# Weighting q before its transposes for the first four token tiles, and pairing the feed-forward units of both token halves

## The chip, the core and the metric

The kernel runs on one core of a Trainium2 chip. Its engines are TensorE (PE in the profile, with its weight loads as PEld), VectorE (DVE), ScalarE (ACT), GpSimd (POOL) and SyncE (SP); each works through its own instructions in order. Data comes from and goes to device memory by DMA, issued from the queues of SP, POOL and, once, ACT. The metric is device time of one execution in microseconds.

## The reference

Attention with a cosine weighting and no softmax, and behind it a gated feed-forward layer:

```python
theta = pi / 2 * arange(S) / S                       # S = 576
phi(x) = concat([relu(x) * cos(theta), relu(x) * sin(theta)], axis=-1)
kv  = einsum('bhsf,bhsd->bhfd', phi(k), v)           # B = 8, H = 8, D = 64
z   = sum over s of phi(k)
x   = einsum('bhsf,bhfd->bhsd', phi(q), kv) / (einsum('bhsf,bhf->bhs', phi(q), z) + 1e-6)
x   = x with the heads side by side: 4608 tokens x 512
out = (silu(x @ w_gate) * (x @ w_val)) @ w_out       # 512 -> 1536 -> 512
```

Inputs and output are float32. The kernel computes in bf16 with float32 sums.

## The kernel before

**Tokens.** A batch's 576 positions are held as 64 partitions times 9 *slots* (position = 9 p + c for partition p and slot c). Two heads, e = 0 and 1, share the 128 partitions; the four head pairs are g = 0 to 3, taken two at a time as j = 0, 1 with i = g mod 2. A *token tile* t is two neighbouring slots of all eight heads, 128 tokens; tile 4 takes the last slot of batch 0 and the first of batch 1. Four tiles make a token group of 512, `tg`, of which there are nine.

**Attention.** `relu_k` makes relu(k), `vmul` multiplies v by cos and sin and appends the weights themselves, so that `kv_mm` gives kv and z in one product; `kv_out` copies it from PSUM into `kvd`, a matrix in which the blocks for other heads are zero. The weights of q are applied late: `qturn_pe` transposes q's slots on PE and the relu that copies them out of PSUM gives `qt`; `a_half(t, j)` multiplies `qt` by `kvd` into 2 x 260 columns, ACT scales the cosine half into `tmp` (L278), and DVE scales the sine half and adds it, giving `num` (L279). `x_norm` divides by the denominator: `den` (L287), `rec` (L289) and `x` in two halves (L293). `x_turn` transposes x on PE (L309), and ACT copies it into `xT` (L310), or, later in the kernel, it does so by DMA.

**Feed-forward.** `ffn_fc(tg, fc, lo, hi)` is a *unit*: for one of 12 column blocks fc, the products with w_gate and w_val (L329) over slots lo to hi of a token group, silu on ACT (`sg`, L337), the product on DVE (`ht`, L339). `ffn_out` multiplies `ht` by w_out (L355) and copies the sum as `ob` (L362), on ACT for even tiles and on DVE for odd ones, for SP to write out.

**PSUM.** All eight banks are one tile; `take(n)` hands them out round robin, n at a time and aligned, skipping those that are held. The kv product is held until `kv_free`, an output sum until its last piece is issued. A bank that is handed out again is written once its earlier readers are through.

**Order.** It is written out by hand. q and v of batch 0 come by SP in float32 (`first_q`, the first `CUT[0]` = 4 slots, and `first_v`), the rest by POOL with a cast to bf16, in the order of the calls: w0, ..., w5 are pairs of column blocks of w_gate and w_val (`load_w`), wo0 to wo2 thirds of w_out (`load_wo`). `idle_products(n)` issues n products of zeros, used by nothing. For token group 0 the units are split into halves: a0 to a11 are the units of tiles 0 and 1, b0 to b11 those of tiles 2 and 3. `order` lists them and `at(slot, ...)` hangs other work behind one; a slot (piece, t) stands behind a third of output tile t. In `order` before, a0 to a5 come first, and then the b units with the rest of a between them; a0 and a1 are themselves split into a quarter for tile 0 and one for tile 1. From token group 1 on, units take 512 tokens. PE takes up everything in this order.

Of the kernel before, what the change touches and what calls it, by code (L numbers as in the profile page):

```python
# [17 lines left out]
def kernel(  # L18
# [10 lines left out]
    nc = tc.nc  # L29
    B, H, S, D = q.shape  # L30
    P = 128
    G = H // 2
    J = G // 2
# [50 lines left out]
    def raw_of(b, nm):  # L84
        if (b, nm) not in raws:
            raws[b, nm] = raw.tile([P, G, NC, D], BF16, name=f"raw_{nm}")
        return raws[b, nm]

    def load(b, nm, parts=1):
        t, sv, n = raw_of(b, nm), source(b, nm), G // parts  # L90
        for i in range(parts):
            sl = slice(i * n, (i + 1) * n)
            nc.gpsimd.dma_start(out=t[:, sl].rearrange("p g c d -> p g (c d)"), in_=sv[:, sl])  # L93

    def load_slots(b, nm, lo, hi):
        nc.gpsimd.dma_start(out=raw_of(b, nm)[:, :, lo:hi].rearrange("p g c d -> p g (c d)"),
                            in_=source(b, nm)[:, :, lo * D:hi * D])
# [4 lines left out]

    def load_first(nm, gs, cs=slice(0, NC)):
        if nm not in first:
            first[nm] = consts.tile([P, G, NC, D], FP32, name=f"first_{nm}")
        nc.sync.dma_start(out=first[nm][:, gs, cs].rearrange("p g c d -> p g (c d)"),  # L106
                          in_=source(0, nm)[:, gs, cs.start * D:cs.stop * D])

# [20 lines left out]
    def idle_products(n):  # L129
        ps = take(1)  # L130
        for _ in range(n):
            nc.tensor.matmul(out=ps, lhsT=zeros, rhs=zeros.unsqueeze(1).to_broadcast([P, 4, P]), start=True, stop=True)  # L132

    idle_products(24)


    rad = math.pi / 2.0 / S
# [48 lines left out]
    def relu_op(eng, out, in_):  # L186
        if eng == "act":
            nc.scalar.activation(out=out, in_=in_, func=AF.Relu)  # L188
        else:
            nc.vector.tensor_single_scalar(out=out, in_=in_, scalar=0.0, op=ALU.max)  # L190

    def relu_k(b, lo, hi, eng):
        o = raw_of(b, "k")[:, lo:hi]
        relu_op(eng, o, o)
# [6 lines left out]
    def vmul(b, g):  # L201
        nc.vector.tensor_tensor(  # L202
            out=v2s[b % 2][:, g, :, :, 0:D],
            in0=(first if b == 0 and g < 2 else {"v": raw_of(b, "v")})["v"][:, g].unsqueeze(2).to_broadcast([P, NC, 2, D]),
            in1=tab, op=ALU.mult,
        )
# [37 lines left out]
    def kv_out(b, engs=("act", "dve"), js=slice(0, J)):  # L244
        ps = st[b, "kvps"]
        for e, eng in enumerate(engs):
            for i in range(2):
                hs = slice(i * D, (i + 1) * D)
                (nc.scalar.copy if eng == "act" else nc.vector.tensor_copy)(  # L249
                    out=kvd[b % 2][hs, e, js, :, i].rearrange("p j w x -> p (j w) x"),  # L250
                    in_=ps[hs, e, js.start * 2 * D1:js.stop * 2 * D1].rearrange("p (y x) -> p y x", x=D1))

    def kv_free(b):
        held.pop(("kv", b))

    xT = {}

# [83 lines left out]
    def ffn_fc(*a):  # L341
        ffn_mm(*a)
        ffn_act(*a)
# [36 lines left out]
                                                        in_=ob[e * SH:(e + 1) * SH, 0:hi - lo])  # L380


    for i in range(5):
        load_w(i)
    load(1, "k")
    load(1, "v", 2)
    load_w(5)
    load_slots(1, "q", 0, CUT[1])
    for i in range(3):
        load_wo(i)  # L390
    load_slots(1, "q", CUT[1], NC)
    for nm in ("k", "v", "q"):
        load(2, nm)

# [4 lines left out]
    def at(s, *fns):  # L399
        plan.setdefault(s, []).extend(fns)  # L400
# [5 lines left out]
    def a_(t, j):  # L406
        return lambda: (a_half(t, j), x_norm(t) if j else None)

    def turn(t, fast=False):
        return lambda: x_turn(t, fast)  # L410

    def q_(b, j, part, eng="act"):
        lo, hi = ((0, CUT[b]), (CUT[b], NC))[part]
        return lambda: qturn_pe(b, j, lo, hi, eng)


    def relu_first_q(j, cs, eng):
        sl = slice(2 * j, 2 * j + 2)
        relu_op(eng, raw_of(0, "q")[:, sl, cs], first["q"][:, sl, cs])

    def relu_first_q(j, eng):
        sl = (slice(None), slice(2 * j, 2 * j + 2), slice(0, CUT[0]))
        relu_op(eng, raw_of(0, "q")[sl], first["q"][sl])

    vmul(0, 0)
    vmul(0, 1)
    for g in (2, 3):
        nc.scalar.copy(out=raw_of(0, "v")[:, g], in_=first["v"][:, g])
        vmul(0, g)
    for j in range(J):  # L430
        relu_first_q(j, "act")
    for j in range(J):
        q_(0, j, 0)()
    relu_k(0, 0, 2, "dve")
    idle_products(2)
    kv_mm(0, 0)
    idle_products(2)
    kv_out(0, js=slice(0, 1))
    relu_k(0, 2, 4, "dve")
    for t in range(2):  # L440
        a_(t, 0)()
    kv_mm(0, 1)
    idle_products(3)
    kv_out(0, js=slice(1, 2))
    kv_free(0)
    for t in range(2):
        a_(t, 1)()
    q_(0, 0, 1)()
    idle_products(6)
    x_turn(0, fast=True)  # L450
    q_(0, 1, 1)()
    idle_products(2)
    for f in range(2):
        ffn_fc(0, f, 0, 2)
    a_(2, 0)()
    x_turn(1, fast=True)
    a_(2, 1)()


    order = [("a", f) for f in range(6)]  # L460
    for f in range(FC):
        order.append(("b", f))
        if f in (0, 1, 3, 4, 7, 8):
            order.append(("a", {0: 6, 1: 7, 3: 8, 4: 9, 7: 10, 8: 11}[f]))
    at("a0", a_(3, 0))
    at("a1", a_(3, 1))
    at("a3", turn(2, True))
    at("a5", turn(3, True))
    at("b2", lambda: relu_k(1, 0, 2, "dve"))
    at("a9", lambda: relu_k(1, 2, 4, "dve"))  # L470
    for g in range(G):
        at(f"b{4 + g}", lambda g=g: vmul(1, g))
    at("a10", lambda: kv_mm(1, 0))
    at("a11", lambda: kv_mm(1, 1), lambda: kv_out(1))
    at("b10", lambda: kv_free(1))
    at("b9", q_(1, 0, 0))
    at("b10", q_(1, 1, 0), a_(4, 0))
    at("b11", a_(4, 1))
    at((0, 0), a_(5, 0), q_(1, 0, 1))
    at((0, 1), a_(5, 1), q_(1, 1, 1))  # L480
    at((0, 2), turn(4, True))
    at((0, 3), a_(6, 0))
    at((1, 0), turn(5, True), a_(6, 1))
    at((1, 2), a_(7, 0), turn(6, True))
    at((1, 3), a_(7, 1))
    at((2, 1), turn(7, True))
    HALF = GH // 2
    for nm, f in order:
        ffn_fc(0, f, *((HALF, GH) if nm == "b" else (0, HALF) if f > 1 else (2, HALF)))
        slot(f"{nm}{f}")  # L490
    for piece in range(3):
        for t in range(OUT):
# [76 lines left out]
```

## Time and profile before

| | us |
|---|---|
| median of 6 runs | 339.83 |
| lowest and highest run | 338.48 and 341.64 |
| the profiled execution, device time | 340.66 |
| its span, first to last instruction | 338.8 |
| PE busy in the span | 328.9 |
| DVE, ACT, POOL busy | 189.3, 158.1, 32.3 |
| first unit of token group 0 starts | 20.00 |
| unit b0 starts | 29.54 |
| token group 1 starts | 63.32 |

The profile counts time from the first instruction. The span is shorter than the device time, which takes in what lies before and after it. Busy time of PE overstates its work, since a matmul's end is modelled and overlaps the next one; what PE truly spends is seen from the starts of successive matmuls.

### The profile page before, as it was taken

Reading aid. Unit: us, or ns where it says so; the run is one execution under the profiler, and the core shown is the slowest. Engines: PE = TensorE matmul, PEld = TensorE weight load, DVE = VectorE, ACT = ScalarE, POOL = GpSimd, SP = SyncE. Lnnn points to the kernel's source line nnn. Section 1 sums busy time; section 2 is a strip of 40 time slices with the busy share of each in tenths; the row PEclk is TensorE's granted clock in tenths of the full one; section 3 lists DMA queues with packets and bytes.
Section 4 is the critical chain, followed back from the end, with each engine's and each line's share of the span. In section 5 each row is a group of like instructions: output and inputs, shape, how many; then the busy total and the mean of one; then the engine's idle time right before and its main releaser. Section 6 shows DMA issues by size and latency. Waiting matters only on the chain.

```text
span 338.8 us, 5965 instructions
## 1 busy us (share of the span) xinstructions
PE 328.9 (97%) x2299; PEld 165.7 (49%) x2299; DVE 189.3 (56%) x426; ACT 158.1 (47%) x309; POOL 32.3 (10%) x50
## 2 busy tenths in 40 slices
PE   8789999999999999999999999999999999999995
PEld 3358865454445444444444444544444445444443
DVE  6385855589725962596259714981478147714320
ACT  6564464678425741584157514851354135413321
POOL 9454320002002000200000000000000000000000
PEclk9999999999999999999999999999999999999999
DMA  8999999998985928492810172017301410141013
GB/s 237 196 197 203 206 206 207 234 220 137 157 157 88 167 38 172 67 183 48 155 41 16 34 149 62 15 31 135 75 18 31 98 44 15 32 110 31 0 33 93
DMA packets 57085, 36.76 MB, mean 109 GB/s; under 512 B 31329, under 2 KB 52065, under 8 KB 57057
## 3 DMA queue, kind: packets, MB, share of 16 engines
q0 software_dynamic: 20624, 18.03, 33.5%
q1 hardware_dynamic: 36272, 18.23, 25.8%
q8 instruction: 18, 0.29, 0.4%
q10 hardware_dynamic: 160, 0.13, 0.1%
q14 instruction: 11, 0.08, 0.1%
HBM read 37.75 MB, written 9.44 MB: 139 GB/s over the span
## 4 chain that ended last, share of the span: by engine, by line
PE 91%; DMA 3%; DVE 2%; ACT 2%; issue 1%; SPq 0%; ACTq 0%
PE banks L329 56%; PE banks L355 26%; PE banks L268 5%; PE banks L237 3%; DMA first_q<-in_q_dram 3%; DVE x L293 1%; DVE num L279 1%; ACT tmp L278 1%; PE banks L223 1%; PE banks L373 0%; PE banks L309 0%; ACT raw_q L188 0%; ACT xT L310 0%; PE banks L132 0%; SPq L106 0%
## 5 line engine op out<-in xcount | busy, mean ns | idle before, releaser
L329 PE MATMUL banks<-xT,wg_sb 128*128 128x512 bf16 (+2 forms) x488 | 113.5, 355 | 2.2 <-DVE ht L339 0.8
L329 PE MATMUL banks<-xT,wv_sb 128*128 128x512 bf16 (+2 forms) x488 | 113.3, 355 | 0.0
L339 DVE TENSOR_TENSOR ht<-sg,banks 128x512 bf16<-128x512 bf16 (+2 forms) x122 | 76.1, 624 | 66.0 <-PE banks L329 50.8
L337 ACT ACTIVATE sg<-banks 128x512 bf16<-128x512 f32 (+2 forms) x122 | 66.9, 548 | 89.9 <-PE banks L329 87.5
L355 PE MATMUL banks<-wo_sb,ht 128*128 128x512 bf16 x420 | 93.6, 379 | 0.0
L329 PEld LDWEIGHTS <-wv_sb 128*128 128x128 bf16 x488 | 47.2, 98 | 46.3
L329 PEld LDWEIGHTS <-wg_sb 128*128 128x128 bf16 x488 | 45.7, 98 | 39.1 <-issue 3.6
L355 PEld LDWEIGHTS <-ht 128*128 128x128 bf16 x420 | 40.7, 98 | 46.4 <-issue 0.4
L362 DVE COPY ob<-banks 128x512 f32<-128x512 f32 x17 | 11.8, 691 | 55.2 <-PE banks L355 55.1
L278 ACT ACTIVATE tmp<-banks,cst 128x260 f32<-128x260 f32 x72 | 34.1, 476 | 15.5 <-PE banks L268 15.4
L279 DVE SCALAR_TENSOR_TENSOR num<-banks,cst,tmp 128x260 f32<-128x260 f32 x72 | 34.8, 484 | 9.2 <-ACT tmp L278 8.9
L362 ACT COPY ob<-banks 128x512 f32<-128x512 f32 x18 | 10.6, 586 | 55.0 <-PE banks L355 55.0
L268 PE MATMUL banks<-kvd,qt 128*128 128x260 bf16 (+1 forms) x160 | 27.8, 276 | 0.4 <-DVE kvd L249 0.2
L293 DVE TENSOR_TENSOR x<-num,rec 128x256 bf16<-128x256 f32 x72 | 27.4, 421 | 1.2
L202 DVE TENSOR_TENSOR v<-raw_v,tab 128x1152 bf16<-128x1152 bf16 x30 | 22.3, 752 | 0.0
L268 PEld LDWEIGHTS <-qt 128*128 128x128 bf16 (+1 forms) x160 | 13.3, 100 | 17.0 <-issue 3.3
L188 ACT ACTIVATE raw_k<-raw_k 128x576 bf16<-128x576 bf16 x24 | 16.0, 675 | 0.0
L188 ACT ACTIVATE r_q<-raw_q 128x576 bf16<-128x576 bf16 x24 | 16.0, 675 | 0.0
L93 POOL DMA_DIRECT2D raw_k<-in_k_dram x9 | 7.0, 780 | 87.1 <-issue 82.7
L132 PE MATMUL banks<-zeros 128*128 128x512 bf16 x39 | 12.3, 469 | 1.0 <-DVE zeros L127 1.0
L237 PEld LDWEIGHTS <-raw_k 64*64 64x64 bf16 x576 | 8.8, 106 | 6.2 <-issue 5.3
L237 PE MATMUL banks<-v,raw_k 64*64 64x130 bf16 x576 | 11.5, 220 | 0.0
(45 smaller groups left out, 98.0 us busy)
## 6 DMA issues: line engine op xcount, KB each, us to landing
out_dram<-ob SPq DMA_DIRECT2D x70, 128.0 KB, 2.4
raw_k<-in_k_dram POOLq DMA_DIRECT2D x7, 576.0 KB, 12.0
raw_v<-in_v_dram POOLq DMA_DIRECT2D x6, 576.0 KB, 13.4
raw_q<-in_q_dram POOLq DMA_DIRECT2D x6, 576.0 KB, 15.5
wg_sb<-in_moe_w_gate_dram POOLq DMA_DIRECT2D x6, 256.0 KB, 10.6
wv_sb<-in_moe_w_val_dram POOLq DMA_DIRECT2D x6, 256.0 KB, 10.8
wo_sb<-in_moe_w_out_dram POOLq DMA_DIRECT2D x3, 512.0 KB, 14.9
first_v<-in_v_dram SPq DMA_DIRECT2D x2, 576.0 KB, 4.1
```

Source lines behind the costliest of these rows:

```text
L188: nc.scalar.activation(out=out, in_=in_, func=AF.Relu)
L202: nc.vector.tensor_tensor(out=v2s[b % 2][:, g, :, :, 0:D], in0=(first if b == 0 and g < 2 else {"v": raw_of(b, "v")})["v"][:, g].unsqueeze ...
L237: nc.tensor.matmul(out=ps[i * D:(i + 1) * D, e, j * 2 * D1:(j + 1) * 2 * D1], lhsT=raws[b, "k"][es, g, c], rhs=v2s[b % 2][es, g, c, :, 0:D ...
L268: nc.tensor.matmul(out=ps[ms, e, 0:4 * D1], lhsT=st[b, "qt"][:, e, j, c:c + n].rearrange("p c s -> p (c s)"), rhs=kvd[b % 2][:, e, j].rear ...
L278: nc.scalar.activation(out=tmp, in_=av[:, :, 0], func=AF.Copy, scale=cst[:, c0, 0:1])
L279: nc.vector.scalar_tensor_tensor(out=st["num", t][:, j], in0=av[:, :, 1], scalar=cst[:, c0, 1:2], in1=tmp, op0=ALU.mult, op1=ALU.add,)
L293: nc.vector.tensor_tensor(out=x[:, 4 * j * D:(4 * j + 4) * D].rearrange("p (i e d) -> p e i d", i=2, e=2), in0=num[:, hs, 0:D].rearrange(" ...
L329: nc.tensor.matmul(out=o, lhsT=w[:, kc, fs], rhs=xT[tg][:, kc, ts], start=(kc == 0), stop=(kc == KC - 1))
L337: nc.scalar.activation(out=sg[:, 0:n], in_=ps[0], func=AF.Silu)
L339: nc.vector.tensor_tensor(out=ht[:, fc, r:r + n], in0=sg[:, 0:n], in1=ps[1], op=ALU.mult)
L355: nc.tensor.matmul(out=o_ps[t], lhsT=ht[:, fc, r:r + P], rhs=wo_sb[:, fc], start=(fc == 0), stop=(fc == FC - 1))
L362: (nc.scalar.copy if t % 2 == 0 else nc.vector.tensor_copy)(out=ob, in_=ps)
```

## The change

For tiles 0 to 3 q is weighted first: `weight_q(c, w, eng)` makes relu(q) times the cosine (w = 0) or sine (w = 1) of one slot in one instruction, on ACT or DVE, into `qw`. `turn_qw(t)` transposes both, and ACT and DVE copy one each into `qwT`. `a_tile(t)` multiplies both by their parts of `kvd` and adds them in PSUM, and DVE divides straight from PSUM with one `den`, one `rec` and one `x` for the tile. The ninth slot of batch 0 still goes through `qturn_pe`, now behind b1. The order becomes pairs, two a units and two b units in turn; all of column blocks 0 and 1 for tiles 0 and 1 comes before it. Loads, v products, kv products and the tiles 4 to 7 hang at other slots, and the numbers of products of zeros differ (24, 2, 2, 3, 6 and 2 before; 28, 2, 4 and 3 after).

```diff
-            first[nm] = consts.tile([P, G, NC, D], FP32, name=f"first_{nm}")
+            first[nm] = consts.tile([P, G, cs.stop, D], FP32, name=f"first_{nm}")
...
-    idle_products(24)
+    idle_products(28)
...
+    NW = 8
+    qw = consts.tile([P, 2, J, NW, 2, D], BF16)
+    qwT = {}
+
+    def weight_q(c, w, eng):
+        o, sc = qw[:, w, :, c], csk[:, c, w:w + 1]
+        i = (first["q"] if c < CUT[0] else raw_of(0, "q"))[:, :, c].rearrange("p (j i) d -> p j i d", i=2)
+        if eng == "act":
+            nc.scalar.activation(out=o, in_=i, func=AF.Relu, scale=sc)
+        else:
+            nc.vector.tensor_scalar(out=o, in0=i, scalar1=sc, scalar2=0.0, op0=ALU.mult, op1=ALU.max)
+
+    def turn_qw(t):
+        qwT[t] = consts.tile([P, 2, 2, J, 2, SH], BF16, name=f"qwT_{t % 2}")
+        for w, eng in enumerate(("act", "dve")):
+            ps = take(1).bitcast(BF16).rearrange("p (y e s) -> p y e s", e=2, s=SH)
+            for j in range(J):
+                for c in range(2):
+                    nc.tensor.transpose(out=ps[:, 2 * j + c].rearrange("p e s -> p (e s)"),
+                                        in_=qw[:, w, j, 2 * t + c].rearrange("p i d -> p (i d)"), identity=ident)
+            (nc.scalar.copy if eng == "act" else nc.vector.tensor_copy)(
+                out=qwT[t][:, w].rearrange("p e j c s -> p (j c) e s"), in_=ps[:, 0:2 * J])
+
+    def a_tile(t):
+        ps = take(2)
+        for e in range(2):
+            for j in range(J):
+                for w in range(2):
+                    nc.tensor.matmul(
+                        out=ps[:, e, 2 * j * D1:2 * (j + 1) * D1],
+                        lhsT=qwT[t][:, w, e, j].rearrange("p c s -> p (c s)"),
+                        rhs=kvd[0][:, e, j, w].rearrange("p i x -> p (i x)"),
+                        start=(w == 0), stop=(w == 1),
+                    )
...
+        nc.vector.tensor_single_scalar(out=dv, in_=num[:, :, :, D:D1], scalar=1e-6, op=ALU.add)
...
+        nc.vector.reciprocal(out=rec, in_=den)
...
+        nc.vector.tensor_tensor(
+            out=x.rearrange("p (y e d) -> p e y d", e=2, d=D), in0=num[:, :, :, 0:D],
...
-    for i in range(5):
+    for i in range(4):
         load_w(i)
     load(1, "k")
+    load_w(4)
+    load_w(5)
     load(1, "v", 2)
-    load_w(5)
     load_slots(1, "q", 0, CUT[1])
-    for i in range(3):
-        load_wo(i)
+    load_wo(0)
+    load_wo(1)
     load_slots(1, "q", CUT[1], NC)
+    load_wo(2)
...
-    for j in range(J):
-        relu_first_q(j, "act")
-    for j in range(J):
-        q_(0, j, 0)()
+    for c in range(CUT[0]):
+        weight_q(c, 0, "act")
+        weight_q(c, 1, "dve")
     relu_k(0, 0, 2, "dve")
-    idle_products(2)
+    turn_qw(0)
     kv_mm(0, 0)
     idle_products(2)
+    relu_k(0, 2, 4, "dve")
+    turn_qw(1)
     kv_out(0, js=slice(0, 1))
-    relu_k(0, 2, 4, "dve")
-    for t in range(2):
-        a_(t, 0)()
     kv_mm(0, 1)
-    idle_products(3)
+    idle_products(4)
     kv_out(0, js=slice(1, 2))
     kv_free(0)
-    for t in range(2):
-        a_(t, 1)()
-    q_(0, 0, 1)()
-    idle_products(6)
+    a_tile(0)
+    a_tile(1)
+    idle_products(3)
+    for c in (4, 5):
+        weight_q(c, 0, "act")
+        weight_q(c, 1, "act")
     x_turn(0, fast=True)
-    q_(0, 1, 1)()
-    idle_products(2)
+    turn_qw(2)
+    for c in (6, 7):
+        weight_q(c, 0, "act")
+        weight_q(c, 1, "dve")
+    a_tile(2)
     for f in range(2):
         ffn_fc(0, f, 0, 2)
-    a_(2, 0)()
     x_turn(1, fast=True)
-    a_(2, 1)()
+    turn_qw(3)
+    for f in range(2):
+        ffn_fc(0, f, 2, 4)
+    x_turn(2, fast=True)
+    a_tile(3)
...
-    order = [("a", f) for f in range(6)]
-    for f in range(FC):
-        order.append(("b", f))
-        if f in (0, 1, 3, 4, 7, 8):
-            order.append(("a", {0: 6, 1: 7, 3: 8, 4: 9, 7: 10, 8: 11}[f]))
-    at("a0", a_(3, 0))
-    at("a1", a_(3, 1))
-    at("a3", turn(2, True))
-    at("a5", turn(3, True))
-    at("b2", lambda: relu_k(1, 0, 2, "dve"))
+    order = []
+    for f in range(0, FC, 2):
+        order += [("a", g) for g in (f + 2, f + 3) if g < FC]
+        order += [("b", g) for g in (f, f + 1)]
+    at("a3", turn(3, True))
+    for j in range(J):
+        at("b1", lambda j=j: qturn_pe(0, j, NC - 1, NC, "act"))
+    at("a8", lambda: relu_k(1, 0, 2, "dve"))
     at("a9", lambda: relu_k(1, 2, 4, "dve"))
-    for g in range(G):
-        at(f"b{4 + g}", lambda g=g: vmul(1, g))
-    at("a10", lambda: kv_mm(1, 0))
-    at("a11", lambda: kv_mm(1, 1), lambda: kv_out(1))
-    at("b10", lambda: kv_free(1))
-    at("b9", q_(1, 0, 0))
-    at("b10", q_(1, 1, 0), a_(4, 0))
-    at("b11", a_(4, 1))
-    at((0, 0), a_(5, 0), q_(1, 0, 1))
-    at((0, 1), a_(5, 1), q_(1, 1, 1))
-    at((0, 2), turn(4, True))
-    at((0, 3), a_(6, 0))
-    at((1, 0), turn(5, True), a_(6, 1))
-    at((1, 2), a_(7, 0), turn(6, True))
+    for g, s in enumerate(("a10", "a11", "b8", "b9")):
+        at(s, lambda g=g: vmul(1, g))
+    at("b9", lambda: kv_mm(1, 0))
+    at("b10", lambda: kv_mm(1, 1), lambda: kv_out(1))
+    at("b11", q_(1, 0, 0), q_(1, 1, 0))
+    at((0, 0), lambda: kv_free(1), a_(4, 0))
+    at((0, 1), a_(4, 1))
+    at((0, 2), a_(5, 0))
+    at((0, 3), a_(5, 1))
+    at((1, 0), turn(4, True), q_(1, 0, 1), a_(6, 0))
+    at((1, 1), a_(6, 1), q_(1, 1, 1))
+    at((1, 2), turn(5, True), a_(7, 0))
     at((1, 3), a_(7, 1))
-    at((2, 1), turn(7, True))
+    at((2, 0), turn(6, True))
+    at((2, 2), turn(7, True))
     HALF = GH // 2
     for nm, f in order:
-        ffn_fc(0, f, *((HALF, GH) if nm == "b" else (0, HALF) if f > 1 else (2, HALF)))
+        ffn_fc(0, f, *((HALF, GH) if nm == "b" else (0, HALF)))
         slot(f"{nm}{f}")
```

More of the change, by code (lines that the diff above doesn't have):

```diff
@@ L254, in kv_free @@
         held.pop(("kv", b))
+    NW = 8
[29 more added lines that the diff above has]
+                    )
+        num = ps[:, :, 0:2 * J * D1].rearrange("p e (y x) -> p e y x", x=D1)
+        den = smp.tile([P, H, 1], FP32, name="den")
+        dv = den.rearrange("p (e y) o -> p e y o", e=2)
+        nc.vector.tensor_single_scalar(out=dv, in_=num[:, :, :, D:D1], scalar=1e-6, op=ALU.add)
+        rec = smp.tile([P, H, 1], FP32, name="rec")
+        nc.vector.reciprocal(out=rec, in_=den)
+        x = xp.tile([P, d_model], BF16, name="x")
+        nc.vector.tensor_tensor(
+            out=x.rearrange("p (y e d) -> p e y d", e=2, d=D), in0=num[:, :, :, 0:D],
+            in1=rec.rearrange("p (e y) o -> p e y o", e=2).to_broadcast([P, 2, 2 * J, D]), op=ALU.mult,
+        )
+        st["x", t] = x
     xT = {}
@@ L414, in q_ @@
         return lambda: qturn_pe(b, j, lo, hi, eng)
[L417 to L423, printed above, removed]
     vmul(0, 0)
```

## The prediction

> **What bounds the kernel now.** Three views, in this order: the busy table and slices, the chain that ended last, and TensorE's timeline around the stages that the diff edits.
>
> ```profile
> PE 328.9 (97%) x2299; PEld 165.7 (49%) x2299; DVE 189.3 (56%) x426; ACT 158.1 (47%) x309; POOL 32.3 (10%) x50
> PE 91%; DMA 3%; DVE 2%; ACT 2%; issue 1%; SPq 0%; ACTq 0%
> ```
>
> TensorE (PE) is the bound: the chain is 91% PE. After 63.32 us no row shows PE waiting, so what the edited part saves comes off the end in full, and only the first 63 us matter. There the chain runs:
>
> ```profile
> 1.75 8.51 DMA first_q<-in_q_dram
> ...
> 18.12 0.77 DVE x L293 x2
> 18.89 0.04 issue
> 18.94 0.29 PE banks L309 x2
> ...
> 28.91 0.59 ACT xT L310
> 29.50 0.04 issue
> 29.54 11.51 PE banks L329 x104
> ```
>
> Nothing starts before q lands at 10.26; the first x is ready at 18.89; PE is dense from 29.54, where unit b0 begins. The stretches from there:
>
> ```profile
> 29.54:47.12 17.58, 17.58 (x232) 14.78 (x232) 10.63 (x25) 8.10 (x21) 7.23 (x10) 1.00 1.29 204
> 47.12:63.32 16.20, 15.67 (x107) 7.84 (x105) 9.81 (x27) 9.02 (x18) 0.74 (x1) 1.00 1.21 208
> ```
>
> (Columns: stretch, length, busy PE, weight loads, DVE, ACT, POOL, clock, DMA share, GB/s.) The first is full. The second, one unit and the twelve output pieces, has holes that busy time partly hides, because a matmul's modelled end overlaps the next:
>
> ```profile
> 56.89 0.39 PE L268 MATMUL banks<-kvd,qt 128*128 128x260 bf16 x2
> 57.43 0.62 PE L309 MATMUL banks<-ident,x 128*128 128x128 bf16 x4
> ...
> 58.97 1.89 PE L355 MATMUL banks<-wo_sb,ht 128*128 128x512 bf16 x8
> 61.13 0.62 PE L309 MATMUL banks<-ident,x 128*128 128x128 bf16 x4 [0.27 <-DVE x L293]
> ```
>
> Two matmuls of 260 columns stream in 0.22, so PE stood 0.32 before 57.43; eight of 512 stream in 1.73, so 0.43 before 61.13. With 0.24 inside each of these turns and 0.17 before 54.95, about 1.4 us are stalls.
>
> **What the Trainium skill says.** "ScalarE: Activation LUTs", What ACT_TABLE_LOAD costs: each per-partition pointer operand adds about 93 ns. The trace agrees: tmp, 128x260 with a pointer scale, 478 ns; sg, 128x256, 384. "VectorE: DVE Perf Modes", the perf-mode tier table: one-source fp32 SBUF operations can run at 2x, those from PSUM at most 2x, tensor_tensor from PSUM at 1x. Agreement: the tab cast, 1152 fp32, took 0.76 (0.16 + 1152 x 0.52 ns); x, 256 from fp32, 421 ns (0.155 + 267). No row shows a bf16 PSUM copy on DVE. "TensorE: Matmul & The Clock Gate", Part 1: the array runs at half clock until some 3.4 us of activity, and again after an idle window of that length. The trace shows the start of it: products of zeros 0.43 apart until 6.9, then 0.22.
>
> **The change, part by part.** *Early stage.* The two relu of q (0.62 each), 32 of 36 q transposes, the four qt relu, eight tmp (0.478) and eight num (0.485) of tiles 0 to 3 go. Added: 16 weightings, 32 transposes of 128 columns (four take 0.22), eight qwT copies, and per tile one den (0.21) and rec (0.20) and one x of 512 instead of two of 256. The matmuls stream the same 16 x 260 columns. Prices: ACT weighting as tmp, 0.48, 0.39 apart; DVE weighting 0.16 + 256 x 0.52 = 0.29, 0.21 apart (1x: 0.42 and 0.34); qwT on ACT as the 128x512 xT copy, 0.58; on DVE between 0.42 (2x) and 0.69 (the fp32 ob copy); x of 512, 0.155 + 533 = 0.69. At the low prices:
>
> - Weightings from 10.28: DVE done 11.20, ACT 11.94. The first k relu (0.46) now queues behind DVE's, to 11.6. Turns of tile 0 on PE 11.22 to 11.66, kv product 11.75 to 12.40, turns of tile 1 12.83 to 13.27, second kv product 13.36 to 14.01, products of zeros to 14.88. Both engines copy qwT, then kvd: ACT to 14.82, DVE to 15.00.
> - Tile 0 multiplies 14.9 to 15.34, tile 1 to 15.78. den, rec, x: x(0) ready 16.7 (before, 18.9), x(1) 17.8.
> - x turn 0 at 16.78, turns of tile 2 to 17.44. Their DVE copy is queued behind x(1), to 18.2, so the product of tile 2 starts 18.35, with the first FFN units behind it in PE's order: 18.79 to 19.67. Turn 1 follows; its xT copy waits for two silus on ACT, 20.1 to 20.7. Second FFN pair 20.73 to 21.6, turn 2, tile 3, a2 and a3 22.26 to 24.0, turn 3. From a turn to a unit on its xT took 28.43 to 29.54 = 1.1 before: b0 at 25.1.
>
> With DVE weighting at 1x the second k relu and all behind it move 0.45; with 0.69 copies 0.25 more: b0 at 25.8. Neither below nor above has a row; I take 25.4.
>
> *Ledger at b0.* 29.54 - 25.4 = 4.14 earlier. But before had a4 and a5 done by then: two units of 0.873 = 1.75 are now behind. Left 2.39. Turning q's ninth slot in b1 is four transposes with switching, 0.33: left 2.06.
>
> *v products.* Four of them now stand on DVE behind a10, a11, b8, b9. Before, ht and v product together took 1.00 a unit:
>
> ```profile
> 40.23 0.75 DVE L202 TENSOR_TENSOR v<-raw_v,tab 128x1152 bf16<-128x1152 bf16 x1
> 40.90 0.41 DVE L339 TENSOR_TENSOR ht<-sg,banks 128x256 bf16<-128x256 bf16 x1
> 41.23 0.75 DVE L202 TENSOR_TENSOR v<-raw_v,tab 128x1152 bf16<-128x1152 bf16 x1
> ```
>
> The first ht comes 1.49 after its unit's start, so the fourth v product ends 1.49 + 3 x 1.00 + 0.34 + 0.75 = 5.58 after a10's start. PE comes to the second kv product at 4 units + 0.09 + 0.65 + 1 unit + 0.09 = 5.2. It waits 0.43, and b11 behind it: left 1.63.
>
> *Output pieces.* Tile 4 moves behind b11, so all four tiles' halves fall into eight pieces. Walked from b11 with rows of before (tmp 0.42 after its matmul, num 0.51 after tmp, 1.12 for den, rec and both x): q turn j=1, part 1, takes bank 2, which tile 6's first num must free (its product streams at 7.8; its tmp stands behind xT of tile 4 and a qt relu on ACT, to 9.04; num to 9.55), PE ready at 9.2: 0.4. In the order in which `take` hands out banks, turn 6 gets bank 4, that of output piece 0, just finished: it waits for the ob copy on ACT, 0.17 + 0.03 + 0.59 + 0.05 = 0.84, and output 1 waits behind it. Turn 7 gets output 2's bank 5: 0.83. The waits for x of tiles 6 and 7 are gone. Stalls 2.07 against 1.4: left **0.96, about 1.0 us**.
>
> *At nothing.* POOL's queue: w4, w5 move around k and v of batch 1. Landings of before, reordered: w4 29.0 (26.3), w5 31.8 (34.7), v 34.6 (32.0); first uses, from b0 = 25.4: a8 34.3, a10 37.8. wo0 lands about 39 for 46, wo1 42 for 51; q's rest passes wo2, which lands 45.5 for 53. A cover of 3 us or more; were it gone, PE waits the difference. SP carries the same first loads. Four more products of zeros at the start end at 10.1, ahead of 11.22; those later lie under kvd copies.
>
> **Sum.** Profiled execution: 340.66, span 338.8, 1.86 around it. Minus 1.0: 339.7. It is 0.83 above the median of the six runs (339.83), so the same gain on the median gives **338.8**.
>
> **Rivals.** *The early gain is kept.* For it: x(0) 2.2 us earlier, and DVE below full everywhere. If the four later waits come to no more than before's 1.4, 2.06 remain, with b0 at 25.1 2.4: 337.6. Against: both bank waits follow from the order of allocation.
> *The clock falls.* Between 16.5 and 19.9 I count some 2.0 us of PE work in 3.4; before's emptiest such stretch, 10.0 to 13.4, shows 2.33 busy. If that counts as idle, one 3.4 us window at half rate costs 1.7 in the units, plus about 1.0 in the turns before: 2.7 lost against 1.0 gained, 341.5. It decides once matmuls of 256 columns start 0.22 apart rather than 0.11. Against: clock 1.00 in all stretches of before.
> *The change doesn't reach the end*: q's landing at 10.26 gates both kernels, but PE's work after it differs, so no tie follows from this alone.
>
> **How the numbers follow.** A measurement can tell about 0.5%, 1.7 us. The walk, gain 0.3 to 1.7: 0.48 (0.07 faster, 0.40 same, 0.01 slower, as the runs of before spread 338.5 to 341.6). Gain kept: 0.35 (0.33 faster, 0.02 same). Clock: 0.17 (0.13 slower, 0.04 same). Faster 0.40, same 0.46, slower 0.14. Range 336.9 to 341.0: the gain kept with 0.7 of spread below, most of the clock's case above; the walk's own is 337.9 to 339.7.
>
> **What would show it.** Right: b0 near 25.4; x(0) near 16.7; turns 6 and 7 on PE each about 0.8 after output 0 and 2, ended by the ob copy on ACT; a wait for v before the second kv product; tile group 1 starting near 62.3 (63.32). Wrong: b0 under 24.6 or over 26.2, no ob waits, or 256-column matmuls 0.22 apart.

## The result: no difference that can be measured

| | before | after |
|---|---|---|
| median, us | 339.16 (72 runs, 338.17 to 342.54) | 339.31 (35 runs, 338.76 to 343.48) |
| ratio, 95% interval | | 1.0001 (0.9986 to 1.0015) |
| the profiled execution: time, span, us | 340.66, 338.8 | 341.88, 340.0 |
| b0 starts, us | 29.54 | 27.62 |
| token group 1 starts, us | 63.32 | 64.55 |
| from there to the end of the span, us | 275.5 | 275.45 |

The forecast was 338.8 with 336.9 to 341.0; the likeliest single outcome, "same", came. The profiled execution of the changed kernel is not a typical one: its start is disturbed, as the second row of the next view shows. Only its later part is compared directly with before; the early part is read from an experiment with the same early part and no disturbance.

The page of the changed kernel, its busy table, the granted clock and DMA in 40 slices, and the chain by engine:

```profile
span 340.0 us, 5993 instructions
...
PE 329.0 (97%) x2313; PEld 168.4 (50%) x2313; DVE 188.9 (56%) x424; ACT 157.9 (46%) x311; POOL 32.3 (10%) x50
...
PEclk9799999999999999999999999999999999999999
DMA  7999999997985928491820172016401420141013
GB/s 228 198 201 199 205 208 207 233 218 119 156 158 86 179 43 157 71 196 35 150 60 16 34 146 64 15 31 123 90 16 31 93 47 15 34 108 31 0 33 93
...
PE 91%; DVE 2%; DMA 2%; ACT 2%; issue 0%; SPq 0%; ACTq 0%
```

PE is still the bound, with the same busy time. Two things are to be seen here for later: the 7 in the clock's second slice, and the DMA engines, which move 200 GB/s or so without a pause through nine slices, that is until about 76 us.

The chain of waits of the changed kernel, in order of time (start, length, what):

```profile
1.75 8.25 DMA first_q<-in_q_dram
10.03 1.32 DVE qw L267 x4
11.35 0.38 DVE raw_k L190
11.78 1.19 PE banks L237 x36
...
14.82 0.42 DVE qwT L277
15.25 0.19 DVE kvd L249
15.46 0.31 DVE kvd L249
15.80 0.72 PE banks L237 x35
...
18.43 0.70 DVE x L298
...
27.62 1.91 PE banks L377 x16
...
45.09 0.68 DVE v L202
45.81 0.71 PE banks L237 x34
...
55.69 0.50 DVE num L327
56.23 0.41 PE banks L223 x8
...
60.05 0.59 ACT ob L410
60.68 0.38 PE banks L357 x4
...
62.83 0.59 ACT ob L410
63.47 0.38 PE banks L357 x4
```

q lands at 10.0; the first kv product (11.78) and the second (15.80) are now separated by copies of qwT and kvd on DVE; b0 is at 27.62. In the later part each wait of the prediction stands on the chain: v before the second kv product of batch 1, num before a turn of q (56.23), and the copies of ob before the turns of tiles 6 and 7. The windows view of the same kernel (stretch, length, busy PE, weight loads, DVE, ACT, POOL, clock, DMA share, GB/s):

```profile
11.60:15.00 3.40, 3.03 (x47) 2.15 (x47) 1.06 (x4) 1.27 (x4) 1.96 (x3) 0.52 1.44 196
15.00:27.62 12.62, 10.25 (x156) 8.36 (x156) 8.42 (x27) 8.42 (x22) 5.27 (x8) 0.99 1.40 200
27.62:46.45 18.83, 18.70 (x228) 15.99 (x228) 11.15 (x25) 7.63 (x21) 7.40 (x10) 1.00 1.30 204
46.45:64.55 18.10, 16.45 (x133) 8.71 (x129) 10.32 (x28) 10.66 (x21) 2.22 (x3) 1.00 1.21 208
```

In this execution the clock stood at half from 11.72 to 15.13. There the kv product took 1.19; in an execution at full clock it takes 0.72 (after_bank, below). From b0 on the clock is full. Executions of most kernels here, before too, come with and without a stretch of half clock (the mean clock is below 0.9965 with it); the medians hold both, and where it matters, runs at full clock are given apart.

### The profile page after: what moved, and what is told of

It is laid out like the page before. It is cut to its first block, busy times and chain, and to the rows that moved or that the text cites. A ratio compares the mean times of both kernels' runs of the same rounds, so it can differ in the third digit from the quotient of the medians.

```text
span 340.0 us, 5993 instructions
## 1 busy us (share of the span) xinstructions
PE 329.0 (97%) x2313; PEld 168.4 (50%) x2313; DVE 188.9 (56%) x424; ACT 157.9 (46%) x311; POOL 32.3 (10%) x50
## 3 DMA queue, kind: packets, MB, share of 16 engines
q1 hardware_dynamic: 36272, 18.23, 25.4%
## 4 chain that ended last, share of the span: by engine, by line
PE 91%; DVE 2%; DMA 2%; ACT 2%; issue 0%; SPq 0%; ACTq 0%
PE banks L377 55%; PE banks L403 27%; PE banks L316 4%; PE banks L237 3%; DMA first_q<-in_q_dram 2%; DVE v L202 1%; PE banks L132 1%; PE banks L357 1%; PE banks L421 0%; PE banks L285 0%; ACT xT L358 0%; DVE ht L387 0%; PE banks L275 0%; PE banks L223 0%; DVE qw L267 0%
## 5 line engine op out<-in xcount | busy, mean ns | idle before, releaser
L410 DVE COPY ob<-banks 128x512 f32<-128x512 f32 x17 | 11.8, 692 | 56.3 <-PE banks L403 56.2
L326 ACT ACTIVATE tmp<-banks,cst 128x260 f32<-128x260 f32 x64 | 30.5, 476 | 13.6 <-PE banks L316 12.8
L410 ACT COPY ob<-banks 128x512 f32<-128x512 f32 x18 | 10.6, 586 | 55.9 <-PE banks L403 55.9
L327 DVE SCALAR_TENSOR_TENSOR num<-banks,cst,tmp 128x260 f32<-128x260 f32 x64 | 31.0, 485 | 7.1 <-ACT tmp L326 6.7
L341 DVE TENSOR_TENSOR x<-num,rec 128x256 bf16<-128x256 f32 x64 | 24.4, 421 | 1.1
L316 PE MATMUL banks<-kvd,qt 128*128 128x260 bf16 (+1 forms) x144 | 24.9, 277 | 0.0
L316 PEld LDWEIGHTS <-qt 128*128 128x128 bf16 (+1 forms) x144 | 11.8, 100 | 15.9 <-issue 3.4
L237 PE MATMUL banks<-v,raw_k 64*64 64x130 bf16 x576 | 12.5, 225 | 1.1 <-ACT kvd L249 0.7
L237 PEld LDWEIGHTS <-raw_k 64*64 64x64 bf16 x576 | 9.6, 109 | 7.2 <-issue 5.8
L132 PE MATMUL banks<-zeros 128*128 128x512 bf16 x37 | 11.0, 455 | 1.0 <-DVE zeros L127 1.0
```

The source lines that it names most:

```text
L237: nc.tensor.matmul(out=ps[i * D:(i + 1) * D, e, j * 2 * D1:(j + 1) * 2 * D1], lhsT=raws[b, "k"][es, g, c], rhs=v2s[b % 2][es, g, c, :, 0:D ...
L316: nc.tensor.matmul(out=ps[ms, e, 0:4 * D1], lhsT=st[b, "qt"][:, e, j, c:c + n].rearrange("p c s -> p (c s)"), rhs=kvd[b % 2][:, e, j].rear ...
L326: nc.scalar.activation(out=tmp, in_=av[:, :, 0], func=AF.Copy, scale=cst[:, c0, 0:1])
L327: nc.vector.scalar_tensor_tensor(out=st["num", t][:, j], in0=av[:, :, 1], scalar=cst[:, c0, 1:2], in1=tmp, op0=ALU.mult, op1=ALU.add,)
L341: nc.vector.tensor_tensor(out=x[:, 4 * j * D:(4 * j + 4) * D].rearrange("p (i e d) -> p e i d", i=2, e=2), in0=num[:, hs, 0:D].rearrange(" ...
L410: (nc.scalar.copy if t % 2 == 0 else nc.vector.tensor_copy)(out=ob, in_=ps)
```

## The experiments

Times are medians; ratios are to before on the same chip, formed over the rounds (they are not the quotients of the medians). In a line of a timeline, the brackets say how long the engine stood before it and for what.

**The changed early part alone** (early_only): before's order and places from b0 on, the changed prologue and loads.

```diff
-    order = []
-    for f in range(0, FC, 2):
-        order += [("a", g) for g in (f + 2, f + 3) if g < FC]
-        order += [("b", g) for g in (f, f + 1)]
+    order = [("a", f) for f in range(2, 6)]
+    for f in range(FC):
+        order.append(("b", f))
+        if f in (0, 1, 3, 4, 7, 8):
+            order.append(("a", {0: 6, 1: 7, 3: 8, 4: 9, 7: 10, 8: 11}[f]))
...
```

> The early part alone: q weighted before its transposes for tiles 0 to 3 and the changed loads, but the unit order and the places of everything behind it as before. Theory A (the early part gains about 2 us, the later places give it back): b11 is reached as in the changed kernel or earlier, no v wait before the second kv product, no ob wait at turns 6 and 7, stalls of about 1.4 us in the output pieces; 1.1 us less than the changed kernel for these, and up to 0.7 more because a4 and a5 now stand between turn 3 and b0: 337.5 us, ratio to before 0.993 to 0.997. Theory B (the early gain is lost in the early part itself, to the clock that fell to half in the profiled execution): ratio 0.998 to 1.003, as the changed kernel. Theory C (the profiled execution of before was a slow one and there is no early gain against its usual run): ratio near 1.000 though the profile shows b0 early.

Measured: 341.83, ratio 1.0052 (1.0031 to 1.0073). The ranges of all three theories lie below this ratio. 18 of its 22 runs have the half clock, 19 of 59 of before's; the four at full clock have a median of 339.63 against 339.08, too few to tell a gain from none. The profiled execution, at full clock, begins group 1 at 60.95, that is 51.22 after its q landed (9.73), where before takes 53.06: 1.84 sooner. It then waits for something that no part of the change touches:

```profile
76.72 0.27 PE L316 MATMUL banks<-kvd,qt 128*128 128x260 bf16 x1
77.46 0.28 PE L316 MATMUL banks<-kvd,qt 128*128 128x260 bf16 x1 [0.47 <-DMA qt<-r_q]
```

This is tile 9 in the timeline of PE: the second of its two products waits for the transposes by DMA of batch 2's q.

**The changed later part alone** (late_only): before's prologue, a0 to a5 ahead of b0, then pairs of units, and the changed places of v (behind the four units that end with b9), the kv products and the tiles 4 to 7.

```diff
-    for f in range(FC):
-        order.append(("b", f))
...
+    for f in range(0, FC, 2):
+        order += [("b", g) for g in (f, f + 1)]
+        order += [("a", g) for g in (f + 6, f + 7) if g < FC]
...
+    at("a8", lambda: relu_k(1, 0, 2, "dve"))
...
+    for g, s in enumerate(("b6", "b7", "b8", "b9")):
+        at(s, lambda g=g: vmul(1, g))
...
+    at((2, 0), turn(6, True))
+    at((2, 2), turn(7, True))
```

> The later places alone: early part and loads as before, a0 to a5 first, then pairs of b and a units, v products behind b6 to b9, kv products, q turns, tiles 4 to 7 and turns where the changed kernel has them. Theory A: slower than before by the 0.43 v wait, the q turn wait and two ob waits of 0.83 each, less the stalls of before that go: 1.1 us, ratio 1.002 to 1.004; turns 6 and 7 wait for the ob copies. Theory B: 1.000, the later waits are matched by what they replace. Theory C: says nothing on this kernel against before, 1.003 as A.

Measured: 340.63, ratio 1.0031 (1.0010 to 1.0053). In its profile b0 begins at 28.46 and group 1 at 63.31, 34.85 later; in before it was 33.78. The later places cost 1.07 us; the prediction had summed 1.10, 0.43 for v and 0.67 for the pieces. The forecast of a loss (1.002 to 1.004) came.

**Banks for the turns of tiles 6 and 7** (after_bank):

```diff
-    at((2, 0), turn(6, True))
...
+    at((2, 0), bank_to(6), turn(6, True))
     at((2, 2), turn(7, True))
+    at((2, 3), bank_to(6))
```

Here `bank_to(n)` sets the bank that `take` hands out next, so that both turns get banks other than those of outputs 0 and 2.

> The changed kernel with turns 6 and 7 in banks 6 and 7 in place of those of outputs 0 and 2 that were just finished, and the rotation set back to where it stood. Theory A: both ob waits of about 0.8 us go, token group 1 starts 1.6 us earlier after b11, about 337.7 us, ratio to before 0.994 to 0.997. Theory B: the span is set elsewhere, and PE waits next for x of tile 7 or xT: under 0.5 us gained, ratio 0.998 to 1.001. Theory C: 1.6 us less than the changed kernel, as A.

Measured: 340.18, ratio 1.0011 (0.9986 to 1.0035); the forecast of a gain missed. The waits for ob are gone: group 1 follows b0 after 35.51 us, against 36.93 in the changed kernel. The end does not come sooner, because PE waits here instead (timeline of PE, then the transposes by DMA):

```profile
79.50 0.28 PE L316 MATMUL banks<-kvd,qt 128*128 128x260 bf16 x1 [2.21 <-DMA qt<-r_q]
```

```profile
L214 SPq DMA_TRANSPOSE qt<-r_q x2: 2143/3954/5766, 65.5 to 67.7; - x2
DMA to landing us min/median/max: 11.5/11.6/11.8
```

(How long the issuing took in ns, and when; then the time from issue to landing.) This run has the changed early part at full clock, and shows where that part lost time:

```profile
10.89 0.72 PE L237 MATMUL banks<-v,raw_k 64*64 64x130 bf16 x36
...
13.48 0.85 PE L237 MATMUL banks<-v,raw_k 64*64 64x130 bf16 x36 [0.88 <-ACT kvd L249]
```

The second kv product stands 0.88 for the copies of the first.

**Before once more** (before_again), unchanged.

> The kernel before once more, for a second profiled execution. Theory C: its span is near 336.7 and the two microseconds against the first one (338.8) lie before 29.5 us, where q lands earlier or PE runs at another clock. Theories A and B: span near 338.8, or if shorter, by something outside the stages that the change touches.

Measured: 339.25, span 337.2, in one execution. q landed at 8.76, in the first profile at 10.26, and the whole early part came that much sooner: b0 at 27.94, group 1 at 61.72. So a profile's b0 is not to be set against another's without q's landing between them. Span minus landing of q is 328.5 and 328.4 in the two, so the difference lies where theory C put it. Tile 9 began at 77.49, and its transposes, issued up to 68.5, took at least 8.9: this execution came to them within a few tenths of their landing.

**The kv products ahead of tile 1's turns** (after_kv):

```diff
-    turn_qw(1)
     kv_out(0, js=slice(0, 1))
     kv_mm(0, 1)
-    idle_products(4)
     kv_out(0, js=slice(1, 2))
+    turn_qw(1)
+    idle_products(2)
     kv_free(0)
```

> The changed kernel with the kvd copies and the second kv product ahead of the turns of tile 1, and 2 products of zeros where 4 were. Theory S (a step that was not counted: the second kv product waits for the kvd copies of the first, and these stand behind the qwT copies of tile 1 on ACT and DVE): the second kv product starts 3.1 us after q's landing in place of 4.2, tile 0's product 4.7 in place of 6.0, x(0) 1.2 us earlier against q. Against S: the second product waits for something else (relu of k), and nothing moves.

Measured: 339.21, span 337.2, in one execution. The second kv product now follows the first almost at once, with 0.19 for k and 0.26 for kvd left of its wait:

```profile
10.46 0.72 PE L237 MATMUL banks<-v,raw_k 64*64 64x130 bf16 x36 [0.36 <-DVE raw_k L190]
...
11.91 0.24 PE L237 MATMUL banks<-v,raw_k 64*64 64x130 bf16 x1 [0.19 <-DVE raw_k L190]
12.41 0.72 PE L237 MATMUL banks<-v,raw_k 64*64 64x130 bf16 x35 [0.26 <-DVE kvd L249]
...
15.80 0.40 PE L357 MATMUL banks<-ident,x 128*128 128x128 bf16 x4
```

From the first kv product to the turn of x(0) it is 5.34 instead of 6.11 (10.89 to 17.00 in after_bank). About half of the 0.77 is seen against q's landing (8.49 here): 7.31 to that turn, 7.70 in after_bank, for the first product itself stood for k in this execution. And again the end does not follow: tile 9 waits 0.36 for the same transposes.

**More products at the start** (after_warm): `idle_products(36)` for 28.

> The changed kernel with 36 products of zeros at the start in place of 28. Theory K (clock): in some executions PE is warm early, the 28 products end near 9.1, the gap until the first q transposes counts as idle and the clock falls to half for one window of 3.4 us, which costs 2 to 2.6 us; with 36 the gap is covered when the warm-up is early (products end near 10.6), so hardly any execution shows a mean clock under 0.996 (one in ten of the changed kernel's first runs, a third of the others' on this chip); spans at full clock as the changed kernel or up to 0.7 more, where the warm-up is late and the products end near 11.6, after q. Against K: the share of executions under 0.996 stays, so the fall comes from a later stretch.

Measured: 340.50, ratio 1.0005 (0.9991 to 1.0020), and none of 22 runs has the half clock, where 16 of 49 of before's have it. The price was forecast at up to 0.7 and is more: the median stands 1.2 us above that of the changed kernel's own runs at full clock (339.25, on another chip). It shows in the timeline: the products of zeros run to 11.5, and the first turn stands behind them (11.53) though q had landed at 8.8.

```profile
3.52 8.17 PE L132 MATMUL banks<-zeros 128*128 128x512 bf16 x30
11.53 0.61 PE L275 MATMUL banks<-ident,qw 128*128 128x128 bf16 x8
```

**Prefetch held back** (bank_gate): after_bank with one small copy on POOL that reads `qt` of batch 2, ahead of batch 4's loads on POOL's queue.

```diff
+    seen = consts.tile([P, 2, 1], BF16, name="seen")
...
+            if b == 4:
+                at(p0 - 2, lambda: nc.gpsimd.tensor_copy(out=seen, in_=st[2, "qt"][:, :, 0, 0, 0:1]))
             if b > 3:
                 for s, nm in ((p0 - 2, "k"), (p0, "v"), (p0 + 2, "q")):
```

> The kernel with other banks for turns 6 and 7, and besides a one-element copy on POOL that reads batch 2's qt ahead of the loads of batch 4, so that these start only when its DMA transposes have landed. Theory F (a floor): the transposes of batch 2's q share the DMA engines with the loads of batch 4, land at 77 to 79.5 us whenever they are issued, and what is gained before that is waited away at tile 9 (2.2 us in the profile without the gate). Then the transposes land within 5 us of their issue, PE waits for none, and the end comes 326 us after q's landing if the clock holds, 2 to 3 us less than the 329.8 of the kernel without the gate; executions at full clock have spans of 335 to 336 (336.7 to 339.1 without). Theory L (the loads are what sets the end, the transposes only show it): batch 4's later loads are missed in their turn, or the wait stays; spans as without the gate.

Measured: 341.64, ratio 1.0047 (1.0027 to 1.0068); 12 of 20 runs have a half clock. PE has no wait for qt any more, since batch 2's transposes land in 4.2 and 4.9 us. The delayed loads (issued from 72.9, in before from 44.8) then lie beside the next transposes, those of group 2's x, and the unit that needs them stands (timeline of PE):

```profile
98.26 1.02 PE L377 MATMUL banks<-xT,wg_sb 128*128 128x512 bf16 x4 [2.36 <-DMA xT<-x]
```

In this profile it is this wait that the half clock follows (99.22 to 102.64), not the start. Theory L came, and F missed.

**All of these together** (best): bank_gate with after_kv's order, a2 to a5 ahead of b0, batch 1's v at b4, b5, a10 and a11, and batch 1's second turn of the later q slots one place later.

> All that the runs so far point to in one kernel: the gate, other banks for turns 6 and 7, q turn j=1 part 1 one slot later, the kvd copies ahead of the turns of tile 1, a2 to a5 ahead of b0, v products behind b4, b5, a10 and a11. Theory F with S: b0 14.9 us after q with a4 and a5 done, group 1 starts near 56.5 where q lands at 9.5, no wait in the output pieces over 0.1 us, no wait at tile 9, spans at full clock of 332 to 333.5, time 334 to 335.5, ratio to before 0.984 to 0.990; a fall of the clock adds 2 us in the executions that have one. Theory L: tile 9 or a later tile waits for DMA; ratio 0.994 to 1.000.

Measured: 339.43, ratio 0.9992 (0.9970 to 1.0015). Theory L came again, and F (0.984 to 0.990) missed. Group 1 begins at 59.87 with q landing at 10.23, 3.4 sooner than in before (63.32 with 10.26), and 3.20 is lost at 97.59, in the same wait for xT.

**The gate behind group 2's x** (before_gate, after_gate, best_gate, best_gate32): the copy on POOL now reads the last column of group 2's xT, so that batch 4's loads stay out of both transposes' way. Batch 5's, which stand behind them on the same queue, are held too (to 100.2 in before_gate, 76.7 in before). The gate was put into before; into after_bank with 36 products at the start; into best, in place of the first gate (as shown), with 36 and with 32.

```diff
-                at(p0 - 2, lambda: nc.gpsimd.tensor_copy(out=seen, in_=st[2, "qt"][:, :, 0, 0, 0:1]))
+                at(p0 - 2, lambda: nc.gpsimd.tensor_copy(out=seen, in_=xT[2][:, 0, T - 1:T]))
```

> The kernel before, with one addition: a copy of one element per partition on POOL that reads the last column of group 2's xT, put ahead of batch 4's prefetch loads on POOL's queue, so that these loads start only when all transposes of batch 2's q and of group 2's x have landed. Theory F (the floor: transposes by DMA slowed by prefetch loads stop whatever comes early): before comes to tile 9 just when its transposes have landed, so it gains little from the gate: ratio to before 0.997 to 1.000, span minus landing of q still 328.4 to 328.6, and the transposes of qt land within 5 us instead of 7 to 8. Theory N (the floor binds before as hard as after): ratio 0.993 to 0.996. Theory L (the loads let through late hold something else, as with the gate on qt): a PE wait for xT or for raw_k of over 1 us and a ratio over 1.003.

> The changed kernel with the x turns of tiles 6 and 7 in the banks 6 and 7, 36 products of zeros at the start for 28, and the gate on xT of group 2 ahead of batch 4's loads. Theory F: with the turns' waits, the halved clock and the floor all taken away, the changed early part is worth what it gives: b0 25.4 us with q landed at 9.3 and 28 products, some 1.2 us later with 36 where q lands before 10.3; group 1 some 35.5 us after b0, then 275.4 us: span 337.0 to 337.7 with no wait for qt or xT over 0.5 us, time 338.8 to 339.5, ratio 0.996 to 0.999. Theory L: the floor only moves again, a wait for xT or a later load of over 1 us, ratio 1.000 to 1.004.

> As after_gate, and in addition: the kvd copies and the second kv product ahead of tile 1's turns, the products of a2 to a5 ahead of b0 with batch 1's v weighted at b4, b5, a10 and a11, and batch 1's second ninth-slot turn of q one slot later. Theory F: x(0) some 1.2 us sooner than in after_gate, no wait of kv_mm for v (0.43) and none of the turn for num (0.3): span 335.0 to 336.0, time 336.9 to 337.9, ratio 0.991 to 0.995. Theory L: the gain ends at a new wait, as it did with the gate on qt (3.2 us for xT): span over 337, ratio 0.997 to 1.001.

> best_gate with 32 products of zeros at the start instead of 36. Theory K (the clock falls where products of zeros end long before the first turns of q): 32 end at about 10.6 us, less than 0.9 us before the first turn in most executions, so few runs fall below 0.996 and the time is 0 to 0.6 us under best_gate's. If the gap that is allowed is shorter than that, a third or more of the runs show a clock under 0.996 and the median lies 1 us or more above best_gate's.

| | median, us | ratio (95%) | group 1 starts | transposes of batch 2's qt, us |
|---|---|---|---|---|
| before_gate | 342.64 | 1.0071 (1.0040 to 1.0103) | 64.24 | 4.2 to 4.7 |
| after_gate | 340.51 | 1.0017 (1.0001 to 1.0034) | 61.61 | 4.2 to 4.8 |
| best_gate | 338.21 | 0.9951 (0.9930 to 0.9972) | 59.26 | 4.2 to 4.8 |
| best_gate32 | 337.23 | 0.9926 (0.9899 to 0.9952) | 57.15 | 5.0 to 5.1 |

No kernel of the four waits for qt, and the last two are faster than before; best_gate32 by 2.5 us. But the gate isn't free. Batch 4's v is now late, and DVE, which works in order, hands that on to PE's units (timelines of before_gate: DVE, then PE):

```profile
111.59 0.76 DVE L202 TENSOR_TENSOR v<-raw_v,tab 128x1152 bf16<-128x1152 bf16 x1 [3.60 <-DMA raw_v<-in_v_dram]
```

```profile
113.00 1.02 PE L329 MATMUL banks<-xT,wv_sb 128*128 128x512 bf16 x4 [1.05 <-DVE ht L339]
```

In best_gate32 the same wait is 1.32. From group 1 to the end it takes 277.55 there, 277.0 in best_gate, 277.2 in after_gate and 277.5 in before_gate, against 275.5 without a gate: some 1.5 to 2.1 us. before_gate has nothing but this price: 2.8 us more than before in the median of 8 runs. Its forecast under the floor, a ratio of 1.000 at most, missed, and so did after_gate's (338.8 to 339.5, by 1.0 us); in both the case of a late load came. best_gate missed its 336.9 to 337.9 by 0.3 us. Of the 50 runs with 36 or 32 products and this gate, one has the half clock. best_gate32 was forecast at 0 to 0.6 us under best_gate and came 1.0 under it (337.23 of 10 runs, 338.21 of 18), at the edge of what these runs can tell; q's landing differs between the two profiles too. No run has best's other edits without a gate, so what the gate gives there is not known. In after_gate it gives nothing that shows: 340.51, where after_warm, with the same 36 products and no gate, has 340.50 (on another chip, and without the other banks).

## Why the prediction was right, point by point

The number was right, though the gain of 1.0 us behind it was not there: one term of its sum was mis-sized by just that much, and one general step does not hold. "Same" takes in gains up to 1.7 us, so it would have come with the 1.0 as well; the result alone does not tell the two apart, the profiles do.

*The later part: right.* From b0 to group 1 the prediction implied 62.3 − 25.4 = 36.9; measured 36.93. The wait for v, forecast at 0.43, is 0.38 (PE comes to the product at 45.43, it runs on at 45.81); the forecast's own terms, 5.58 less 5.2, give 0.38 too. The turns of tiles 6 and 7 stand 0.83 and 0.84 by the starts of PE's instructions (outputs 0 and 2 stream out at 59.85 and 62.63, the turns begin at 60.68 and 63.47), both ended by ob on ACT; forecast 0.84 and 0.83. The q turn stands 0.47, forecast 0.4. late_only has the same waits alone and loses the 1.07 us.

*The early part: mis-sized by 1.0 us.* Set against the landing of q, b0 comes 19.28 after it in before (19.18 in before_again, 19.17 in late_only) and 16.13 after it with the changed prologue at full clock (after_bank: 9.30 and 25.43). That is 3.15 sooner, not 4.14. Moved to q's landing at 10.26, after_bank's first kv product would stand at 11.85 (forecast 11.75), tile 1's turns at 12.94 (12.83), the second kv product at 14.44 (13.36), x(0)'s turn at 17.96 (16.78), and b0 at 26.4 (25.4). So the sign that the prediction named for being wrong, b0 over 26.2, came, and group 1 would stand at 63.3, not at 62.3. The step that failed is one: "second kv product 13.36 to 14.01". The walk let it follow tile 1's turns at once; it waits for the kvd copies of the first product (0.88 in after_bank), with which it shares its two banks, and these stand on ACT and DVE behind tile 1's qwT copies. The four weightings on DVE took 1.14 to 1.32, between the two prices named (0.92 at 2x, 1.44 at 1x), but that moved the first kv product by 0.1 only. after_kv puts the copies ahead of the turns and gets 0.77 of it back; after_gate and best_gate, which differ in this and start from the same 36 products, have 6.10 and 4.91 from the first kv product to the turn of x(0).

*The ledger with that one term put right*: 3.15 early, less 1.75 and 0.33, is 1.07; less 0.43 and 0.67 it is −0.03. The change gives and takes the same amount, and "same" needs no other cause. early_only agrees: its 1.84 is this 1.07 and some 0.7 that b0 stands for tile 3's xT in after_bank, where in early_only a4 and a5 lie between. All this is read from single executions, with after_bank for the changed start at full clock.

*"What the edited part saves comes off the end in full": wrong as a rule.* In the changed kernel it was not tried, since nothing was saved: from group 1 to the end it takes 275.45, before 275.5. The variants that did save tried it. The rows of before show no PE wait after 63.32, but they don't show how near one was. The transposes of batch 2's q share DMA with the prefetch of batch 4, and land shortly after its last load, whenever they are issued:

| | issued | batch 4's last load landed | transposes landed | tile 9 needs them | waits |
|---|---|---|---|---|---|
| before | 67.9, 70.1 | 74.9 | 76.9 | 79.1 | none |
| before_again | 66.3, 68.5 | 75.7 | 77.4 | 77.5 | none |
| after | 69.1, 71.0 | 75.3 | 77.2 | 80.3 | none |
| early_only | 65.5, 67.6 | 75.9 | 77.4 | 77.0 | 0.47 |
| after_kv | 65.7, 67.7 | 76.0 | 77.5 | 77.2 | 0.36 |
| after_bank | 65.5, 67.7 | 76.7 | 79.5 | 77.3 | 2.21 |

A transpose issued two microseconds sooner took about two more, because it ends 1.5 to 2.7 after the loads' stream: the 200 GB/s of the page until about 76 us. Where that stream was held back by the gate, the same transposes took 4.2 to 5.1. Why after_bank's came 2 us later than early_only's stays open; its loads account for 0.8 of that. The Trainium skill, "DMA: Bandwidth & Descriptors", Queues, rings and completion order, says that a DMA engine takes turns between its queues packet by packet; that agrees with a transpose slowed by a factor of two and a half beside loads (4.5 against 11.6), though no run here looks at packets. From tile 9's wait to the end takes 259.6 in early_only (77.46 to 337.1) and after_bank (79.50 to 339.1), so in such an execution a landing at 77.4 means a span of 337 and a time near 339, whatever came before. Against q's landing, early_only, after_bank and after_kv begin group 1 1.84, 1.42 and 0.38 sooner than before and then lose these 0.47, 2.21 and 0.36: the last two lose their whole gain, and early_only's profile keeps most of its own (it ends 327.3 after q, before 328.5). Whether the same floor holds before's own executions when q lands early is not shown; its runs go down to spans of 336.3, so the landing isn't at 77.4 in all of them. Medians at full clock show no gain either: 339.08 to 339.23 for before in three comparisons, 339.25 for the changed kernel, 339.28 for after_bank.

*"The clock falls": the mechanism exists, the place and the effect on the comparison were wrong.* It was forecast for 16.5 to 19.9; the profiled execution has it from 11.72 to 15.13, after a gap with no product at all from 9.12 to 10.66. It costs 1.5 us up to b0 (17.62 after q's landing against 16.13). But before's runs have it too, 49 in 155 over three comparisons, 3 in 36 of the changed kernel's own. It hangs on the pause between the products of zeros and q: with 36 products for 28 (after_warm) none of 22 runs has it, where best, with 28 on the same chip, has it in 9 of 14, and early_only and after_bank, with the changed kernel's start, in 26 of 44. The Trainium skill, "TensorE: Matmul & The Clock Gate", Part 1, says that activity is judged by a free-running window of 4096 cycles. The trace's clock record has 3.413 us at half speed, which is 4096 cycles at the 1.2 GHz the page gives for it, after 6.827 us, twice that, at full speed; a free-running window fits that a kernel has it in some executions only. If the changes of the clock mark the ends of such windows, the one that ended at 11.72 began at 8.31, and PE was busy for 1.60 us of it. Counted in the same way, half clock followed windows with 1.05 (bank_gate, 95.81 to 99.22), 1.32 (best) and 1.69 busy (before_gate), and did not follow others with 1.52 (best_gate, near its end), 1.67 (bank_gate, 7.06 to 10.48) and 1.89 (late_only). A window need not be empty, then; which share is enough no run settles. Why early_only has it in 18 of 22 runs while after_bank, with the same prologue, has it in 8 of 22, stays open.

*The other rivals.* "The early gain is kept" fell with the mis-sized term: there were 1.07 us to keep, not 2.06, and the later waits came as forecast. "The change doesn't reach the end" suspected a tie at q's first landing. A later landing ties the ends of some variants; in the changed kernel, whose profile has no wait at tile 9, it had no part.

*"POOL's queue at nothing": held.* No load that the change reordered ends a PE wait in any profile.

## What to carry to other kernels

A row without waits says that nothing is late now, not that nothing is late next: before counting a gain through to the end, take every transfer behind the edit whose landing is set by bandwidth and not by its issue, and measure its slack (here 2.2 us in one execution of before and 0.1 in the next, for a gain of 1 to 2). In a walk along one engine, ask of each product which bank it writes and who must still read there; those copies queue behind whatever was put on their engine in the meantime. And set profiles of a start against each other from the landing of the first input, not from zero.

## What the runs showed of the hardware that was not expected

The first q lands between 7.5 and 10.6 us after the first instruction, in executions of kernels that load it in the same way. The transposes by DMA of batch 2's q took 4.2 to 5.1 us with the prefetch loads held back and up to 11.8 beside them. Holding these loads back costs later what it saves, in part: batch 4's v lands 13 us after its issue (98.7 to 111.6 in before_gate), and a unit waits 1.05 for it, in best_gate32 1.32. And half clock does not need a whole window of 3.4 us without work: one with 1.6 us of products and a gap of 1.5 was followed by it. Every stretch of the clock record between two changes inside the run is a multiple of 3.413 us: 6.827 at full speed and 3.413 at half in the profiles of the changed kernel, best and before_gate, and in bank_gate 95.573 (28 times) up to the stall for xT.
